# Queries and keys of the last nine blocks turned by DMA instead of by TensorE, in a fused attention and MLP kernel

## The chip, the cores and the metric

The kernel runs on one core of a Trainium2 chip. The metric is the time of one execution on the device, in microseconds (us). A kernel is timed in several runs; one execution is profiled as well. The engines' names are those of the profile: PE is TensorE's matmul side, PEld its weight loads, DVE is VectorE, ACT is ScalarE, POOL is GpSimd, SP is SyncE. In this kernel SP only issues DMAs, and POOL issues the loads and makes a few small vectors.

## The reference

Attention with a sliding window and a linear distance penalty, then a normalized MLP with a residual. There are 8 batches, 8 heads, 576 tokens and 64 dimensions a head.

```python
scores = scale * np.matmul(q, k.transpose(0, 1, 3, 2))
mask = (rel >= 0) & (rel < 128)                  # rel = query position - key position
scores = np.where(mask, scores + bias[None], -1000000000.0)   # bias = -slope_h * |rel|
...
attn = attn / (np.sum(attn, axis=-1, keepdims=True) + 1e-09)
out = np.matmul(attn, v)
...
xn = (x - mu) / np.sqrt(var + 1e-06) * g_ln      # x: heads joined, 512 wide
ch = np.maximum(xn @ w_ch1, 0.0) @ w_ch2         # 512 -> 2048 -> 512
return x + ch
```

## The kernel before

**Blocks.** The batches are taken in 4 pairs. The 576 tokens of a batch are four strips of 128 and a tail of 64. A pair has 9 blocks of 128 queries: two for each strip (one per batch) and one for both tails. `order` (L229) lists the 36 blocks, n = 9 * pair + block; "the last nine blocks" are n = 27 to 35, all of pair 3. The 36 blocks form groups for the MLP (`GROUPS`, L26): six groups of two blocks, then six of four.

**Turning.** A score matmul contracts over the 64 dimensions of a head, so q and k must lie with the dimensions on the partitions; two heads share the 128 partitions. `load_qk` (L207) has POOL issue the loads of a strip for both batches: the DMA converts to fp16 and puts pairs of neighbouring tokens side by side, so that one load has 512 pieces of 128 numbers. `turn` (L283) then has PE transpose 64x64 pieces against an identity (`transposed`, L267, the matmuls are on L277): 64 for a strip, 32 for a tail. They go to PSUM, from the ninth block on mostly to the two banks `ps_sc` that the scores use too, and DVE and ACT copy them to SBUF (L296, L297, for a tail L302), where keys come back to token order and queries keep all even tokens ahead of the odd ones. `turned_pool` has three buffers for q and three for k.

**Attention.** `scores` and `attend` (L367) compute a block's scores in 64x64 quadrants of PE (L393): j is the half of the array's rows (the head of a pair), c the half of its columns. Each of the 128 queries sees only the keys in its window, so `seen` (L353) leaves out halves of queries that no mask lets through; what stays in the bank from earlier is finite, and the mask makes it zero. Only for the first eight blocks is everything computed. ACT takes the exponential from PSUM (L401), DVE multiplies by the decayed mask (L412), PE multiplies by v with a column of ones (`values`, L431, matmuls on L445), and DVE divides by the sum (L454).

**Normalization.** From block 8 on, `stats` (L494) makes mean and variance on DVE (L542, L543) and the reciprocal deviation rstd on POOL (L497, L500); `normal` (L480), called centring here, subtracts the mean and multiplies by rstd on DVE (L484) and has SP issue a DMA transpose of the 128x512 block into the group's tile xT (L492).

**MLP.** `mlp1(g)` multiplies xT by the first weights (L677): 16 units of 128 hidden columns, 4 matmuls each; ACT (some on DVE) applies the maximum with zero (L693). `mlp2` (L701) is the second product for the small groups (L710). For groups 6 to 11 `fast_mlp2` (L747) does it with seven products of half size instead of eight (L776), with sums of hidden halves that DVE makes into the buffers `hsum` (L745); it has 14 units. DVE adds the residual, and SP stores the rows (`store`, L862).

**Order.** PE, DVE and ACT run in the order written by hand; the order of POOL is the scheduler's, and before the change SP's too. `steps` is a list of attention steps. For each block n from 8 on it holds four:

```python
steps.append(turn_step(n + 3, True) if ... order[n + 3][1] % 2 == 0 else [])
steps.append(step)        # loads ahead, values(n), scores(n + 2)
steps.append(masks + [(stats, n)])
steps.append([(normal, n)])
```

`weave_at` (L875) interleaves them with the units of the MLP: the numbers in its call say after which unit of that MLP the next step is issued. `mlp1(7)`, for instance, has steps after its units 0, 2, 5, 7, 8, 10, 13 and 15. While the MLP of a group runs, the attention is at the blocks of the next groups; the last steps end in group 10, and group 11 is MLP alone.

**Loads.** The raw q and k have four buffers each, and POOL runs ahead of the other engines: a strip's load is issued when the turn four strips earlier has read its buffer.

Of the kernel before, what the change touches and what calls it, by code (L numbers as in the profile page):

```python
# [10 lines left out]
FP16 = mybir.dt.float16  # L11
# [6 lines left out]
P = 128  # L18
# [9 lines left out]

NV = 10
AHEAD = 6  # L30

# [27 lines left out]
def kernel(  # L59
# [25 lines left out]
    raw_pool = pool("raw", 4)  # L85
    turned_pool = pool("turned", 3)
    probs_pool = pool("probs", 4)
# [41 lines left out]
    g_row = consts.tile([P, DM], FP32)  # L129
    one_line = consts.tile([1, P], FP32)  # L130
# [7 lines left out]
    w2 = consts.tile([P, NFB, DM], FP16)  # L138
    QF, QD = NFB // 2, DM // 2
    hsum = [consts.tile([P, QF, 2 * P], FP16, name=f"hs{i}", tag=f"hs{i}") for i in range(2)]  # L140
    spare = [w1[:, i, :].rearrange("p (f d) -> p f d", d=QD) for i in range(4)]
# [63 lines left out]
    raw = {}  # L205

    def load_qk(src, tag, p, i):  # L207

        n = min(P, S - i * P)
        t = raw_pool.tile([P, H, 2, D], FP16, tag=tag, name=tag)  # L210
        raw[tag, p, i] = t
        for b in range(2):
            nc.gpsimd.dma_start(  # L213
                out=t[b * n // 2 : (b + 1) * n // 2],
                in_=src[2 * p + b, :, i * P : i * P + n, :].rearrange(
                    "h (c r) d -> c h r d", r=2
                ),
            )
# [64 lines left out]
    def turn(p, i, in_sc=False, copies=(nc.vector.tensor_copy, nc.scalar.copy)):  # L283
# [3 lines left out]


        ps = [bank(b if in_sc else None) for b in range(2)]
        k = keys_tile("k", p, i)  # L290
        if i < 4:
            q = queries(p, i)
            transposed("q", p, i, [t[:, 0] for t in ps])
# [4 lines left out]
        else:  # L298
            q = keys_tile("q", p, i)
            for tag, t, dst, copy in zip("qk", ps, (q, k), copies):  # L300
# [10 lines left out]
    def queries(p, i):  # L311
        t = turned_pool.tile([P, 2, 2, HP, HALF], FP16, tag="q", name="q")
        turned["q", p, i] = t.rearrange("p b r h c -> p b h r c")
        return t
# [38 lines left out]
    def seen(p, blk, o, t):  # L353
# [13 lines left out]
    def attend(p, blk, keys, mask, tag, hps):  # L367
# [12 lines left out]
        else:  # L380
            pr = weights_of[p, blk][-1][0]
        banks = ps_sc[len(scored) % 2]
        scored.append((p, blk))
        ps = banks.rearrange("p j (n t q) -> p j n t q", n=len(hps), t=nk)
        qt, b = turned["q", p, blk // 2], blk % 2
        for n, hp in enumerate(hps):
            for t, o in enumerate(keys):
                kt = turned["k", p, o // 2][:, o % 2]
                for c, r, queries in seen(p, blk, o, t):
                    cols = slice(c * HALF, (c + 1) * HALF)  # L390
                    for j in range(2):
                        rows = slice(j * HALF, (j + 1) * HALF)
                        nc.tensor.matmul(  # L393
                            in_halves(ps[cols, j, n, t, :])[:, r, queries],
                            kt[rows, hp, cols],
                            in_halves(qt[rows, b, hp])[:, r, queries],
                            start=True,
                            stop=True,
                        )
        dst = pr[:, heads].rearrange("p h t q -> p h (t q)")  # L400
        nc.scalar.activation(  # L401
# [514 lines left out]
    assert done == len(steps)  # L916
# [30 lines left out]
```

## Time and profile before

| what | value |
| --- | --- |
| median of 3 runs | 323.09 us (323.06 to 325.91) |
| the profiled execution | 322.94 us |
| its span, first to last instruction | 321.1 us |
| granted TensorE clock, mean | 1.00 |
| busy: PE, DVE, ACT, POOL | 307.5, 233.4, 184.6, 114.9 us |
| transposes of q and k on PE (L277) | 528 + 512 to the score banks, 48 + 64 to others |
| transposes of xc by DMA (L492) | 28 |
| bytes by DMA | 32.34 MB in 102048 packets |

A row of the profile's groups gives line, engine, operation, the tiles written and read, and the count; then busy time and the mean of one in ns; then the engine's idle time just before, and what ended it. In a timeline a row is one or more instructions in a run: start and length in us, then what and how many. In a row of waits stand the total, the number of times and the longest. In a table of stages each engine's busy time is followed by its instruction count. "SPq" and "POOLq" are the queues of the two engines, with their DMA issues.

### The profile page before, as it was taken

To read this page: it belongs to the slowest core of one execution; us is meant where nothing else is said; L and a number is where in the kernel's file an instruction comes from. 1 tells how busy PE (TensorE), PEld (TensorE's weight loads), DVE (VectorE), ACT (ScalarE), POOL (GpSimd) and SP (SyncE) were. 2 spreads that over 40 slices of the span, in tenths; PEclk is the share of its full clock that TensorE was granted. 3 is DMA by queue.
4 is the path that set the end of the run, shared out by engine and by line. 5 is a ranking of instruction groups with operands and counts; after the bars stand their busy time and mean duration, and the time that the engine had idled before them with its cause. 6 is when DMAs were issued, how large, how long until landed. Compare 5 with 4: busy or idle time off the path is not lost.

```text
span 321.1 us, 10472 instructions
## 1 busy us (share of the span) xinstructions
PE 307.5 (96%) x4478; PEld 207.3 (65%) x4478; DVE 233.4 (73%) x556; ACT 184.6 (57%) x320; POOL 114.9 (36%) x188
## 2 busy tenths in 40 slices
PE   8889999999899999999999999999999999999993
PEld 2478655758558576545875587558755874685582
DVE  2788878786687788758994899579958984761462
ACT  6588756666558466478248824873488247405600
POOL 8833657769145264534252534220000001000000
PEclk9999999999999999999999999999999999999999
DMA  9999999999999899895389769660340134015005
GB/s 113 169 206 196 190 142 189 186 115 184 59 118 120 78 143 92 89 160 55 45 108 160 68 68 115 117 51 18 84 85 18 18 68 98 18 32 117 0 2 131
DMA packets 102048, 32.34 MB, mean 101 GB/s; under 512 B 92913, under 2 KB 97649, under 8 KB 102002
## 3 DMA queue, kind: packets, MB, share of 16 engines
q0 software_dynamic: 79872, 18.36, 66.7%
q1 hardware_dynamic: 21810, 13.05, 19.5%
q8 instruction: 35, 0.57, 0.8%
q10 hardware_dynamic: 320, 0.26, 0.4%
q14 instruction: 11, 0.09, 0.1%
HBM read 36.90 MB, written 9.44 MB: 144 GB/s over the span
## 4 chain that ended last, share of the span: by engine, by line
PE 76%; DVE 10%; ACT 5%; POOL 3%; DMA 2%; issue 2%; POOLq 0%; ACTq 0%
PE ps_r L677 24%; PE ps_r L776 21%; PE ps_m L710 10%; PE ps_m L677 9%; PE ps_sc L393 4%; ACT probs L401 3%; PE ps_sc L277 2%; PE ps_r L445 2%; DVE probs L412 2%; DMA k<-in_k_dram 2%; PE ps_pv L445 2%; DVE st L542 1%; POOL rstd L500 1%; POOL q L213 1%; DVE o L852 1%
## 5 line engine op out<-in xcount | busy, mean ns | idle before, releaser
L677 PEld LDWEIGHTS <-w1g 128*128 128x128 f16 x640 | 60.0, 98 | 48.9 <-issue 1.8
L677 PE MATMUL ps_r<-xT,w1g 128*128 128x512 f16 x384 | 85.5, 379 | 0.0
L401 ACT ACTIVATE probs<-ps_sc 128x1024 f16<-128x1024 f32 x56 | 54.3, 1027 | 35.5 <-PE ps_sc L393 35.5
L693 ACT ACTIVATE ht<-ps_r 128x512 f16<-128x512 f32 x96 | 56.2, 600 | 30.6 <-PE ps_r L677 30.4
L497 POOL TENSOR_TENSOR rstd<-moments,powers 128x1 f32<-128x1 f32 x28 | 5.4, 193 | 118.5 <-DVE moments L543 118.4
L710 PE MATMUL ps_m<-w,ht 128*128 128x512 f16 x192 | 46.0, 380 | 0.0
L776 PE MATMUL ps_r<-w,ht 128*128 128x256 f16 x384 | 44.1, 273 | 0.0
L223 POOL DMA_DIRECT2D vx<-in_v_dram x40 | 34.6, 879 | 22.4 <-PE ps_r L445 9.7
L412 DVE TENSOR_TENSOR probs<-probs,m 128x1024 f16<-128x1024 f16 x56 | 37.3, 688 | 6.5 <-ACT probs L401 6.3
L776 PEld LDWEIGHTS <-ht 128*128 128x128 f16 x384 | 37.1, 98 | 4.7
L693 ACT ACTIVATE ht<-ps_m 128x256 f16<-128x256 f32 x91 | 33.1, 388 | 8.6 <-PE ps_m L677 6.0
L213 POOL DMA_DIRECT2D q<-in_q_dram x40 | 27.4, 692 | 14.4 <-PE ps_sc L277 6.6
L677 PE MATMUL ps_m<-xT,w1g 128*128 128x256 f16 x256 | 31.4, 273 | 1.1 <-ACT ht L693 0.8
L213 POOL DMA_DIRECT2D k<-in_k_dram x40 | 26.8, 684 | 6.7 <-DMA w<-in_moe_w_ch_dram 3.1
L710 PEld LDWEIGHTS <-ht 128*128 128x128 f16 x192 | 17.1, 98 | 17.4
L484 DVE TENSOR_SCALAR xc<-x,moments,rstd 128x512 f16<-128x512 f16 x28 | 11.5, 412 | 20.0 <-POOL rstd L500 19.0
L542 DVE BATCH_NORM_STATS2 st<-x 128x6 f32<-128x512 f16 x36 | 24.6, 684 | 0.0
L393 PE MATMUL ps_sc<-q,k 64*64 64x128 f16 (+1 forms) x1088 | 20.2, 208 | 3.9 <-DVE k L297 1.3
L296 ACT COPY q<-ps_sc 128x512 f16<-128x512 f16 x15 | 8.8, 586 | 25.1 <-PE ps_sc L277 24.9
L776 PE MATMUL ps_r<-w,hs 128*128 128x256 f16 x192 | 22.5, 273 | 0.0
L445 PEld LDWEIGHTS <-probs 128*128 128x128 f16 x448 | 18.7, 97 | 4.7 <-DVE probs L412 0.3
L393 PEld LDWEIGHTS <-k 64*64 64x64 f16 x1088 | 15.2, 107 | 8.9 <-issue 6.5
(85 smaller groups left out, 390.7 us busy)
## 6 DMA issues: line engine op xcount, KB each, us to landing
out_dram<-o SPq DMA_DIRECT2D x68, 128.0 KB, 2.5
q<-in_q_dram POOLq DMA_DIRECT2D x32, 128.0 KB, 4.5
k<-in_k_dram POOLq DMA_DIRECT2D x32, 128.0 KB, 5.8
vx<-in_v_dram POOLq DMA_DIRECT2D x32, 128.0 KB, 7.6
w<-in_moe_w_ch_dram POOLq DMA_DIRECT2D x8, 512.0 KB, 12.2
q<-in_q_dram POOLq DMA_DIRECT2D x8, 64.0 KB, 4.8
k<-in_k_dram POOLq DMA_DIRECT2D x8, 64.0 KB, 4.3
vx<-in_v_dram POOLq DMA_DIRECT2D x8, 64.0 KB, 6.0
```

The costliest lines, as they stand in the source:

```text
L213: nc.gpsimd.dma_start(out=t[b * n // 2 : (b + 1) * n // 2], in_=src[2 * p + b, :, i * P : i * P + n, :].rearrange("h (c r) d -> c h r d", ...
L223: nc.gpsimd.dma_start(out=vx[p0 : p0 + n, :, 0:D], in_=v[b, :, t0 : t0 + n, :].rearrange("h p d -> p h d"),)
L393: nc.tensor.matmul(in_halves(ps[cols, j, n, t, :])[:, r, queries], kt[rows, hp, cols], in_halves(qt[rows, b, hp])[:, r, queries], start=Tr ...
L401: nc.scalar.activation(out=dst.rearrange("p (n j) q -> p j n q", j=2), in_=ps.rearrange("p j n t q -> p j n (t q)"), func=AF.Exp, scale=in ...
L412: nc.vector.tensor_tensor(out=dst, in0=dst, in1=mask, op=ALU.mult)
L445: nc.tensor.matmul(ps[:, i, :], pr[:, h, t, :], vext[(p * NSLOT + o) % NV][:, h, :], start=(n == 0), stop=(n == len(terms) - 1),)
L484: nc.vector.tensor_scalar(out=xc, in0=xs[order[n]], scalar1=moments[:, n, 0:1], scalar2=rstd[:, n : n + 1], op0=ALU.subtract, op1=ALU.mult,)
L542: nc.vector.bn_stats(out=st, in_=xs[order[n]])
L677: nc.tensor.matmul(ps[:, 0:cols], w[:, kb, fb * P : (fb + 1) * P], xT[:, kb, 0:cols], start=(kb == 0), stop=(kb == NKB - 1),)
L693: nc.scalar.activation(out=ht[:, fb, 0:cols], in_=ps[:, 0:cols], func=AF.Relu)
L710: nc.tensor.matmul(sums[at], ht[:, fb, at * P : (at + 1) * P], w2[:, fb, :], start=(fb == 0), stop=(fb == NFB - 1),)
L776: nc.tensor.matmul(banks[name][pair][:, pair, :], lhs[:, fb, pair * P : (pair + 1) * P], rhs[:, fb, :], start=(first and fb == 0 and (pair ...
```

## The change

For pair 3 (`by_dma(p)`, p >= 3) the loads lay q and k out with tokens on partitions and the heads of a batch side by side, and `turn` has SP issue DMA transposes straight into the turned tiles: two for q and two for k of a strip, one each for the tails, 18 in all. No transposes on PE, no PSUM and no copies are used for them. A strip's q is loaded by four DMAs (even tokens to partitions 0 to 63, odd ones to 64 to 127), so that the queries come in the same order as before, its k by two; pieces are now 64 numbers long.

The turn's place in the steps changes for all pairs: it was the first step of block n + 1, behind the centring of block n; now it stands between `stats(n)` and `normal(n)`. A turn by DMA is issued one block earlier still (n + 5 beside n). SP is under the written order too. A few places of the weave are shifted by one to four units.

`junk` notes for each score bank that transposes were put there; the next scores in that bank compute everything for row half j = 0, which is the half that shares its bank with them. For this the loop over j now stands outside the loop over the columns' halves, in all blocks. `turned_pool` has four buffers instead of three, and the two tiles with g's values are put into the memory of `hsum`.

```diff
@@
+BY_DMA_TURN = 3
...
-    turned_pool = pool("turned", 3)
+    turned_pool = pool("turned", 4)
...
-    g_line = consts.tile([1, DM], FP32)
...
+    g_line, g_row = (
+        t.rearrange("p f d -> p (f d)")[:, 0 : 2 * DM].bitcast(FP32) for t in hsum
+    )
+    g_line = g_line[0:1]
...
+    def by_dma(p):
+        return p >= BY_DMA_TURN
+
     def load_qk(src, tag, p, i):
...
+        if by_dma(p):
+            t = raw[tag, p, i] = t.rearrange("p h r d -> p (h r d)").rearrange(
+                "p (b h d) -> p b h d", b=2, h=H
+            )
+            for b in range(2):
+                rows = src[2 * p + b, :, i * P : i * P + n, :]
+                if i == 4:
+                    parts = [(t[b * n : (b + 1) * n, 0], rows)]
+                elif tag == "k":
+                    parts = [(t[:, b], rows)]
+                else:
+                    rows = rows.rearrange("h (c r) d -> h r c d", r=2)
+                    parts = [
+                        (t[r * HALF : (r + 1) * HALF, b], rows[:, r]) for r in range(2)
+                    ]
+                for dst, part in parts:
+                    nc.gpsimd.dma_start(out=dst, in_=part.rearrange("h p d -> p h d"))
+            return
...
+        k = keys_tile("k", p, i)
+        q = queries(p, i) if i < 4 else keys_tile("q", p, i)
+        if by_dma(p):
+            for tag, dst in (("q", q), ("k", k)):
+                src = raw.pop((tag, p, i))
+                for b in range(2 if i < 4 else 1):
+                    t = dst[:, b]
+                    if tag == "q" and i < 4:
+                        t = turned["q", p, i][:, b].rearrange("p h r c -> p h (r c)")
+                    nc.sync.dma_start_transpose(
+                        out=t, in_=src[:, b].rearrange("p h d -> p (h d)")
+                    )
+            return
...
+        junk[sc] = True
...
+    junk = [False, False]
...
-        if p == 0 and blk < SEEN:
+        if whole or p == 0 and blk < SEEN:
             return [(0, both, every), (1, both, every)]
...
-                for c, r, queries in seen(p, blk, o, t):
-                    cols = slice(c * HALF, (c + 1) * HALF)
-                    for j in range(2):
-                        rows = slice(j * HALF, (j + 1) * HALF)
+                for j in range(2):
+                    rows = slice(j * HALF, (j + 1) * HALF)
+                    for c, r, queries in seen(p, blk, o, t, junk[at] and j == 0):
+                        cols = slice(c * HALF, (c + 1) * HALF)
...
+        junk[at] = False
...
+    def turn_at(n):
+        ahead = [m for m in (n + 3, n + 4) if m < count and order[m][1] % 2 == 0]
+        return [
+            f
+            for m in ahead
+            if by_dma(order[m][0]) == (m == n + 4)
+            for f in turn_step(m, True)
+        ]
+
+    steps.append(turn_at(8))
     for n in range(8, count):
         first_half, second_half = values_steps(n)
-        steps.append(
-            turn_step(n + 3, True) if n + 3 < count and order[n + 3][1] % 2 == 0 else []
-        )
...
+        if n + 1 < count:
+            steps.append(turn_at(n + 1))
         steps.append([(normal, n)])
...
-    with tc.manual_schedule(engines={engine.PE}):
+    with tc.manual_schedule(engines={engine.PE, engine.SP}):
...
-            weave_at(mlp2(3), 0, 1, 1, 2, 4, 4, 5, 6)
+            weave_at(mlp2(3), 0, 1, 1, 3, 4, 4, 5, 6)
...
-            weave_at(mlp2(4), 0, 2, 2, 3, 5, 7, also=(1, 4, 6))
-            weave_at(mlp1(5), 0, 1, 4, 8, 10, 12, also=(3, 6, 9))
+            weave_at(mlp2(4), 0, 2, 2, 5, 5, 7, also=(1, 4, 6))
+            weave_at(mlp1(5), 0, 5, 5, 8, 10, 12, also=(3, 6, 9))
...
-                weave_at(fast_mlp2(g), 1, 3, 6, 7, 7, 9, 12, 13)
+                weave_at(fast_mlp2(g), 1, 3, 6, 7, 7, 10, 12, 13)
```

More of the change, by code (lines that the diff above doesn't have):

```diff
@@ L126 @@
     nc.sync.dma_start(out=g_sb, in_=moe_g_ln.rearrange("(kb p) -> p kb", p=P))
-    g_line = consts.tile([1, DM], FP32)
+    QF, QD = NFB // 2, DM // 2
+    hsum = [consts.tile([P, QF, 2 * P], FP16, name=f"hs{i}", tag=f"hs{i}") for i in range(2)]
+    g_line, g_row = (
+        t.rearrange("p f d -> p (f d)")[:, 0 : 2 * DM].bitcast(FP32) for t in hsum
+    )
+    g_line = g_line[0:1]
     nc.sync.dma_start(out=g_line, in_=moe_g_ln.rearrange("(o d) -> o d", o=1))
-    g_row = consts.tile([P, DM], FP32)
     one_line = consts.tile([1, P], FP32)
@@ L138 @@
     w2 = consts.tile([P, NFB, DM], FP16)
-    QF, QD = NFB // 2, DM // 2
-    hsum = [consts.tile([P, QF, 2 * P], FP16, name=f"hs{i}", tag=f"hs{i}") for i in range(2)]
     spare = [w1[:, i, :].rearrange("p (f d) -> p f d", d=QD) for i in range(4)]
@@ L283, in turn @@
     def turn(p, i, in_sc=False, copies=(nc.vector.tensor_copy, nc.scalar.copy)):
+        k = keys_tile("k", p, i)
[11 more added lines that the diff above has]
+            return
         ps = [bank(b if in_sc else None) for b in range(2)]
-        k = keys_tile("k", p, i)
         if i < 4:
-            q = queries(p, i)
             transposed("q", p, i, [t[:, 0] for t in ps])
@@ L298, in turn @@
         else:
-            q = keys_tile("q", p, i)
             for tag, t, dst, copy in zip("qk", ps, (q, k), copies):
@@ L311, in queries @@
     def queries(p, i):
+        if by_dma(p):
+            t = turned_pool.tile([P, 2, HP, 2, HALF], FP16, tag="q", name="q")
+            turned["q", p, i] = t
+            return t
         t = turned_pool.tile([P, 2, 2, HP, HALF], FP16, tag="q", name="q")
@@ L348, with seen @@
     weights_of, unmasked, scored = {}, {}, []
+    junk = [False, False]
     def in_halves(t):
         return t if len(t.shape) == 3 else t.rearrange("p (r c) -> p r c", r=2)
-    def seen(p, blk, o, t):
+    def seen(p, blk, o, t, whole):
         both, every = slice(0, 2), slice(0, HALF)
         first, second = slice(0, HALF // 2), slice(HALF // 2, HALF)
-        if p == 0 and blk < SEEN:
+        if whole or p == 0 and blk < SEEN:
             return [(0, both, every), (1, both, every)]
@@ L381, in attend @@
             pr = weights_of[p, blk][-1][0]
-        banks = ps_sc[len(scored) % 2]
+        at = len(scored) % 2
+        banks = ps_sc[at]
         scored.append((p, blk))
```

## The prediction

> **What bounds the kernel now.** I read the profile page first, then busy time by stage, then the chain of waits.
>
> ```profile
> span 321.1 us, 10472 instructions
> ...
> PE 307.5 (96%) x4478; PEld 207.3 (65%) x4478; DVE 233.4 (73%) x556; ACT 184.6 (57%) x320; POOL 114.9 (36%) x188
> ```
> ```profile
> 75.00:135.00 60.00, 56.84 (x1002) 38.89 (x1002) 45.39 (x108) 36.79 (x71) 29.17 (x49) 1.00 1.02 106
> 135.00:190.00 55.00, 54.24 (x730) 35.70 (x729) 43.26 (x93) 33.83 (x50) 21.15 (x36) 1.00 1.02 97
> 190.00:256.00 66.00, 65.86 (x1057) 46.15 (x1056) 53.72 (x117) 38.13 (x56) 12.46 (x25) 1.00 0.42 64
> ```
>
> The stage rows give the window, then busy time of PE, PEld, DVE, ACT and POOL, the granted clock, and the DMA share. PE is the bound, and most strictly so where the change works: from 190 to 256 us it idles 0.14 us of 66, at a granted clock of 1.00. From 135 to 190 it idles 0.76 us, from 75 to 135 it idles 3.16 us. So in the last pair a microsecond taken off PE is a microsecond off the end, and elsewhere at most those idle times can be won. "x32" of a PE row is a count of matmuls.
>
> **The turns that leave PE.** The chain of waits runs through all five turns of pair 3; busy time by stage, cut at their starts and ends and for the transposes' line alone (window, PE busy, PEld busy, clock, DMA):
>
> ```profile
> 190.06:190.71 0.65, 0.65 (x64) 0.53 (x64) 1.00 0.00 0
> ...
> 253.55:254.17 0.62, 0.62 (x32) 0.51 (x32) 1.00 0.00 0
> sum 3.33, PE 3.25 PEld 2.70; mean PE 0.65 PEld 0.54
> ```
>
> Four turns of 64 transposes and the tail's 32 (288 in all) take 3.3 us, other matmuls standing right before and behind. All of it goes: **-3.3 us**. With them go nine copies each from DVE and ACT; I give these nothing, because neither engine is the bound after 190 us (DVE is busy 53.72 of 66 us there, ACT 38.13) and PE covers them.
>
> **Waits behind the copies.** After a turn the next scores need its PSUM banks back. These are PE's longest waits from 75 to 135 us, then those from 135 to the end (total, times, longest), and the chain into one of them (start, duration).
>
> ```profile
> PE ps_m L677 <- ACT ht L693: 0.8, 2, 0.5
> PE ps_sc L393 <- DVE k L297: 0.7, 1, 0.7
> PE ps_sc L393 <- DVE rec L453: 0.6, 1, 0.6
> ```
> ```profile
> PE ps_sc L393 <- DVE rec L453: 0.4, 1, 0.4
> PE ps_sc L393 <- DVE k L297: 0.4, 1, 0.4
> ```
> ```profile
> 163.40 0.57 POOL rstd L500
> ...
> 164.00 0.41 DVE xc L484
> ...
> 165.53 0.42 DVE q L296
> 165.94 0.65 DVE k L297
> ```
>
> The chain shows the cause: on DVE the centring (xc) stands ahead of the turn's copies and itself waits for POOL's rstd. The change swaps the two: the copies fill the time in which rstd is made, and turns that stay on PE in pair 2 come two or three units of MLP earlier (a unit is one 128-column slice of hidden, or a quarter of an output block, some 0.9 us) while the scores stay where they were. So both late waits should go: **-0.8 us**. Of the early 0.7 + 0.6 = 1.3 us I take nine tenths, **-1.2 us**, and not more, because PE's other wait there, 0.8 us for ACT's ht, has nothing to do with the copies and is late next. Bounds: none of it, or all 3.16 us idle.
>
> **More scores on PE.** After a turn through the score banks the first scores in each bank now compute all columns in row half 0 (j = 0). Nine such turns remain on PE behind block 8. Pair 0 already computes all columns in both halves; a block of it beside one of pair 2, each with the row that follows it:
>
> ```profile
> 41.46 0.64 PE L393 MATMUL ps_sc<-q,k 64*64 64x128 f16 x32
> 42.04 1.04 PE L710 MATMUL ps_m<-w,ht 128*128 128x512 f16 x4
> ```
> ```profile
> 198.39 0.54 PE L393 MATMUL ps_sc<-q,k 64*64 64x64 f16 x32
> 198.86 0.60 PE L677 MATMUL ps_r<-xT,w1g 128*128 128x512 f16 x2
> ```
>
> Start to next start: 0.58 against 0.47 us, so 0.11 more for both halves. For one half it lies between 0.05 and 0.11; the halves run side by side, so I take 0.09: 9 x 0.09 = **+0.8 us**.
>
> The loops are also turned round, for every block: the four 64x64 quadrants were visited column by column, alternating row halves; now row half 0 twice, then row half 1 twice. Nothing in before runs scores so. But the transposes of a full turn are written in exactly the new order, and 64 of them take 0.65 us, 10 ns each, so the order does not keep quadrants from running together. A tail turn stays in one row half, and there 32 take 0.62 us, 19 ns each. The bounds for the order are thus nothing and, where short matmuls wait for long ones as if all were long, 28 blocks (n from 8) x 0.11 = 3.1 us. I take **+0.5 us**, near the row of the full turn. Sharing g's rows with the hidden sums' buffer, and one turned buffer more, add no instruction, and g's last reader is block 3's centring, long before the first hidden sum: 0. SP's other DMAs keep their order: 0. Of the weave's other places only block 9's values and block 11's scores come later, by one unit, with other matmuls to fill it: 0.
>
> [...]
>
> **What the new path costs: POOL, SP, DMA.** These queues are hidden behind PE unless they come too late. The rows (the landing row is that of xT's 28 transposes, the last two are two of them being issued on SP):
>
> ```profile
> L223 POOL DMA_DIRECT2D vx<-in_v_dram x40 | 34.6, 879 | 22.4 <-PE ps_r L445 9.7
> ...
> L213 POOL DMA_DIRECT2D q<-in_q_dram x40 | 27.4, 692 | 14.4 <-PE ps_sc L277 6.6
> ...
> q<-in_q_dram POOLq DMA_DIRECT2D x32, 128.0 KB, 4.5
> ...
> vx<-in_v_dram POOLq DMA_DIRECT2D x32, 128.0 KB, 7.6
> ```
> ```profile
> 132.97 1.42 POOL L213 DMA_DIRECT2D q<-in_q_dram  x2 [0.89 <-PE ps_sc L277]
> ...
> 138.85 0.25 POOL L497 TENSOR_TENSOR rstd<-moments,powers 128x1 f32<-128x1 f32 x1
> ```
> ```profile
> DMA to landing us min/median/max: 2.4/3.6/7.5
> ```
> ```profile
> 88.31 1.20 SPq L492 DMA_TRANSPOSE xT<-xc  x1
> ```
> ```profile
> 158.36 1.19 SPq L492 DMA_TRANSPOSE xT<-xc  x1
> ```
>
> POOL: a full turn's loads are now four of q with 512 pieces each (priced as the old q load, 0.69 us) and two of k in the shape of v's (0.88): 4.5 us instead of 4 x 0.69 = 2.8, so +1.7 us four times, about 7 us with the tail. Queued behind them is rstd: the one at 138.85 stands behind the loads that begin at 132.97 and would come up to 1.7 us later, still for a block of the group whose MLP starts at 167. Cost 0; if DVE, which waits in order for rstd, has nothing else to do, up to 1.7 us per turn.
>
> Loads lead by far: those from 132.97 are of block 27, which is turned at 190 now and near 176 after; even 7.6 us to land, v's median, leaves over 25 us.
>
> [...]
>
> SP: 18 transposes more at 1.2 us are 21.6 us of queue, in bursts of 4.8 us, put ahead of the transposes of xc for blocks 22, 24, 26, 28 and 30 and of the stores behind them. None of these is the last of its group of four, so each has several units left. A turn's own readers, scores of block 27 say, stand 19 units (some 17 us) behind its issue; 4.8 + 7.5 = 12.3 us at the slowest landing. Cost 0.
>
> **Centring comes one place later.** The MLP of a group needs its last block's xT. The transposes quoted above from 88.31 and 158.36 are the last ones of the groups of blocks 8-9 and 16-19; the matmuls that read them begin here:
>
> ```profile
> 94.99 1.26 PE L677 MATMUL ps_m<-xT,w1g 128*128 128x256 f16 x9
> ```
> ```profile
> 167.11 1.25 PE L677 MATMUL ps_r<-xT,w1g 128*128 128x512 f16 x5
> ```
>
> There are 6.7 and 8.7 us from issue to need, less 3.6 us median landing: 3 and 5 us to spare. Moved behind a turn's two DVE copies (1.07 us) or three units (2.6 us, of which DVE lags some already), they still fit. Cost 0; if not, the difference, in each of six groups.
>
> **Sum.** -3.3 - 0.8 - 1.2 + 0.8 + 0.5 = -4.0 us. The profiled execution took 322.94 us (span 321.1 and 1.8 around it), 0.15 under the median 323.09, so it stands for it: **318.9 us**.
>
> **Rivals.**
> *A, the gain is given back in PE itself:* order and extra columns at their upper bounds, 3.1 + 1.0, and no early wait won: 322.94 - 3.3 - 0.8 + 4.1 = 322.9. Against it, the full turn's 10 ns. A half of this, about 321, is more probable than all.
> *B, slower:* the new order makes scores run as the tail turn does, one row half at a time. If a block's 0.47 us doubles, 28 blocks add 13 us: 318.4 + 13 = 331. It makes the kernel slower than before from 0.16 us a block (4.5 / 28). For it: 19 ns in the tail's turn; against it: the full turn, in the same order. [...]
> *C, a new wait for xT or rstd:* a burst on SP together with a landing of 7.5 us makes the last xT of a group late, 3.9 us past the median and 1.5 of place, so about 0.5 us past the 5 to spare, and more as PE gets ahead by 4; three groups of the last pair at 1 us: about 322. For it: DVE is 53.72 busy of 66 us. Against: after 190 us the DMA share is 0.42, less than half of that before it.
> *D, the transposes were covered anyway:* excluded by 0.14 us idle.
>
> **Numbers.** Forecast 0.60; A 0.18; B 0.08; C 0.14. One per cent, 3.2 us, is about what a measurement tells from no change: faster means under 319.9. The forecast's case spreads from 316.0 (order free, columns at 0.05, all 3.16 idle won: 322.94 - 3.3 - 0.8 - 3.2 + 0.5 = 316.1) to 319.9; A and C lie in 320 to 323, half of B is over 326. So faster 0.59, same 0.31, slower 0.10, range 316.0 to 322.6.
>
> **What would show it.** In the profile after: no transposes of q and k on PE for the last nine blocks and PE time from 190 us to the end shorter by 3.3; 18 more transposes on SP of about 1.2 us; no wait of scores for k's copy; scores of pairs 1 to 3 start to start at 0.47 to 0.50, and 0.56 right after a turn. Scores of 0.6 us or more in all blocks would make B true; PE waiting for the xT DMA, or PE idle behind a centring that waits for rstd, would make C true. The forecast is wrong at its first term if PE idles over 1 us in the last pair.

## The result and the profile after

| what | before | after |
| --- | --- | --- |
| median, first comparison (6 runs each) | 323.41 us | 319.86 us (318.48 to 320.81) |
| ratio | | 0.9878, interval 0.9837 to 0.9919 |
| median, repeated with the experiments | 324.11 us (11 runs) | 319.42 us (6 runs, 318.27 to 320.43) |
| ratio | | 0.9849, interval 0.9819 to 0.9880 |
| profiled execution, span | 322.94, 321.1 us | 320.09, 318.3 us |

The forecast was 318.9 us, in a range of 316.0 to 322.6. The profiled execution after is 2.85 us shorter than the one before, where the sum said 4.0. Ratios leave out a run that is over 1.5% above the fastest of its kernel; of all runs told of here this is one, of two_pairs_pool. In the new kernel the scores are on L434, the transposes of q and k on L301 (PE) and L322 (DMA), the centring on L526 with its DMA transpose on L534, rstd on L539 and L542, the first MLP product on L728, the second on L761 and L827. ACT's maximum is on L744, the copies of the turns on L331 and L332, the moments on L585, the division on L495 and L496, DVE's sums of the second product on L845 and L903, the loads that POOL issues on L234, L237 and L247. The page and the table of stages (window, then PE, PEld, DVE, ACT and POOL, then clock, DMA share and GB/s):

```profile
span 318.3 us, 9920 instructions
...
PE 304.7 (96%) x4190; PEld 205.4 (65%) x4190; DVE 228.9 (72%) x547; ACT 179.4 (56%) x311; POOL 124.7 (39%) x196
```
```profile
0.00:20.00 20.00, 15.73 (x262) 7.52 (x263) 9.27 (x39) 12.78 (x27) 15.88 (x25) 0.91 1.43 153
...
75.00:135.00 60.00, 56.65 (x985) 38.77 (x984) 46.13 (x107) 37.65 (x73) 29.97 (x50) 1.00 1.00 102
135.00:190.00 55.00, 55.00 (x761) 36.15 (x760) 43.06 (x92) 33.89 (x50) 31.03 (x47) 1.00 1.39 114
190.00:256.00 66.00, 66.00 (x807) 46.73 (x805) 52.67 (x117) 34.75 (x49) 12.48 (x23) 1.00 0.59 89
```

PE has 288 matmuls fewer, as it should, and from 135 to 256 us it never idles: the late waits are gone. From 75 to 135 us it still idles 3.35 us, before it was 3.16. And the clock in the first 20 us reads 0.91, where it was 1.00. These are PE's longest waits from 75 to 135 us in the kernel after:

```profile
PE ps_m L761 <- ACT ht L744: 1.2, 1, 1.2
PE ps_m L728 <- DVE x L496: 0.9, 1, 0.9
PE ps_m L728 <- ACT ht L744: 0.6, 2, 0.3
PE ps_m L728 <- DMA xT<-xc: 0.4, 1, 0.4
```

No score waits there for k's copy any more, which was the purpose of the swap, but other waits of the same size have come, among them one for xT. Where the time went is seen best from landmarks. The table gives the time from the first MLP matmul of one group to that of the next, read from the timeline of PE in each trace ("again" is a second profile of the unchanged new kernel; the kernels to the right are those of the experiments below):

| groups | before | after | again | swap_only | dma_only | dma_only_pool | pool_written | before_pool |
| --- | --- | --- | --- | --- | --- | --- | --- | --- |
| 3 to 4 | 19.72 | 19.39 | 19.35 | 19.55 | 19.79 | 18.56 | 17.52 | 18.47 |
| 4 to 5 | 19.66 | 20.50 | 20.58 | 20.32 | 19.74 | 19.74 | 19.89 | 19.67 |
| 5 to 6 | 20.23 | 20.14 | 20.13 | 20.13 | 20.18 | 20.18 | 20.11 | 20.22 |
| 6 to 7 | 32.23 | 31.55 | 31.56 | 31.56 | 32.46 | 32.45 | 31.56 | 32.24 |
| 7 to 8 | 31.75 | 31.02 | 31.01 | 31.95 | 39.60 | 31.02 | 31.01 | 32.12 |
| 8 to 9 | 31.72 | 29.96 | 29.96 | 31.58 | 29.96 | 29.97 | 29.96 | 32.00 |
| 9 to 10 | 31.67 | 30.20 | 30.20 | 31.85 | 30.19 | 30.19 | 30.20 | 31.70 |
| start of group 0 | 19.50 | 20.81 | 19.18 | 19.12 | 21.12 | 21.27 | 19.34 | 19.80 |

The reader is to see three things. The last pair (7 to 10) gives 3.96 us, the same to 0.02 us in every kernel of the table that turns it by DMA, with the one exception of 39.60. The groups 3 to 6 give nothing: 59.61 us before, 60.03 after. And the start varies by some 2 us (19.12 to 21.27) between kernels that run the same matmuls there.

### The profile page after: what moved, and what is told of

The parts are those of the page before. It is cut to its first block, busy times and chain, and to the rows that moved or that the text cites. A ratio compares the mean times of both kernels' runs of the same rounds, so it can differ in the third digit from the quotient of the medians.

```text
span 318.3 us, 9920 instructions
## 1 busy us (share of the span) xinstructions
PE 304.7 (96%) x4190; PEld 205.4 (65%) x4190; DVE 228.9 (72%) x547; ACT 179.4 (56%) x311; POOL 124.7 (39%) x196
## 4 chain that ended last, share of the span: by engine, by line
PE 84%; DVE 5%; POOL 3%; ACT 2%; DMA 2%; issue 2%; POOLq 0%; ACTq 0%
PE ps_r L728 26%; PE ps_r L827 23%; PE ps_m L761 11%; PE ps_m L728 10%; PE ps_sc L434 5%; PE ps_r L487 3%; PE ps_sc L301 2%; PE ps_pv L487 2%; ACT probs L443 2%; DMA k<-in_k_dram 2%; POOL q L237 1%; DVE o L903 1%; DVE x L496 1%; PE ps_warm L283 1%; DVE probs L454 1%
## 5 line engine op out<-in xcount | busy, mean ns | idle before, releaser
L728 PEld LDWEIGHTS <-w1g 128*128 128x128 f16 x640 | 60.4, 98 | 50.5 <-DVE x L496 1.8
L728 PE MATMUL ps_r<-xT,w1g 128*128 128x512 f16 x384 | 85.1, 379 | 0.0
L744 ACT ACTIVATE ht<-ps_r 128x512 f16<-128x512 f32 x96 | 56.2, 600 | 31.6 <-PE ps_r L728 31.5
L761 PE MATMUL ps_m<-w,ht 128*128 128x512 f16 x192 | 46.0, 380 | 1.2 <-ACT ht L744 1.2
L539 POOL TENSOR_TENSOR rstd<-moments,powers 128x1 f32<-128x1 f32 x28 | 6.8, 243 | 102.4 <-DVE moments L585 102.4
L827 PE MATMUL ps_r<-w,ht 128*128 128x256 f16 x384 | 44.1, 273 | 0.0
L247 POOL DMA_DIRECT2D vx<-in_v_dram x40 | 34.7, 884 | 22.3 <-PE ps_r L487 9.0
L827 PEld LDWEIGHTS <-ht 128*128 128x128 f16 x384 | 37.1, 98 | 4.8
L744 ACT ACTIVATE ht<-ps_m 128x256 f16<-128x256 f32 x91 | 32.9, 391 | 8.6 <-PE ps_m L728 6.2
L728 PE MATMUL ps_m<-xT,w1g 128*128 128x256 f16 x256 | 31.5, 273 | 2.2 <-DVE x L496 0.9
L761 PEld LDWEIGHTS <-ht 128*128 128x128 f16 x192 | 17.1, 98 | 18.7 <-issue 1.3
L237 POOL DMA_DIRECT2D q<-in_q_dram x30 | 20.5, 692 | 19.3 <-PE ps_sc L301 10.6
L237 POOL DMA_DIRECT2D k<-in_k_dram x30 | 20.2, 686 | 4.8 <-DMA w<-in_moe_w_ch_dram 3.5
L434 PE MATMUL ps_sc<-q,k 64*64 64x128 f16 (+1 forms) x1088 | 20.5, 210 | 1.5 <-ACT probs L443 1.1
L827 PE MATMUL ps_r<-w,hs 128*128 128x256 f16 x192 | 21.9, 273 | 0.0
L827 PEld LDWEIGHTS <-hs 128*128 128x128 f16 x192 | 18.8, 98 | 2.2
L845 DVE TENSOR_TENSOR o<-ps_r,x 128x512 f32<-128x512 f32 x24 | 16.5, 686 | 4.3 <-PE ps_r L827 4.3
L434 PEld LDWEIGHTS <-k 64*64 64x64 f16 x1088 | 15.2, 108 | 6.8 <-issue 4.6
```

The source lines that it names most:

```text
L237: nc.gpsimd.dma_start(out=t[b * n // 2 : (b + 1) * n // 2], in_=src[2 * p + b, :, i * P : i * P + n, :].rearrange("h (c r) d -> c h r d", ...
L247: nc.gpsimd.dma_start(out=vx[p0 : p0 + n, :, 0:D], in_=v[b, :, t0 : t0 + n, :].rearrange("h p d -> p h d"),)
L434: nc.tensor.matmul(in_halves(ps[cols, j, n, t, :])[:, r, queries], kt[rows, hp, cols], in_halves(qt[rows, b, hp])[:, r, queries], start=Tr ...
L728: nc.tensor.matmul(ps[:, 0:cols], w[:, kb, fb * P : (fb + 1) * P], xT[:, kb, 0:cols], start=(kb == 0), stop=(kb == NKB - 1),)
L744: nc.scalar.activation(out=ht[:, fb, 0:cols], in_=ps[:, 0:cols], func=AF.Relu)
L761: nc.tensor.matmul(sums[at], ht[:, fb, at * P : (at + 1) * P], w2[:, fb, :], start=(fb == 0), stop=(fb == NFB - 1),)
```

## The experiments

My theory after the result was: the five turns give what they were priced at, the swap of turn and centring gives the late waits, and the early waits are kept by POOL, because the scheduler put loads of q and k between a centring's moments and its rstd. The rivals: that the price lies in the new loop order or the extra columns, and that the place of the turn is itself what makes the new waits.

**The DMA turns alone (dma_only).** The turns stand again behind the preceding centring, and the weave has its old places.

```diff
-        if n + 1 < count:
-            steps.append(turn_at(n + 1))
         steps.append([(normal, n)])
+        if n + 1 < count:
+            steps.append(turn_at(n + 1))
```

> Pair 3 is turned by DMA as in the changed kernel, but every turn stands behind the preceding block's centring again, with the old places of the weave. Theory (PE is full from 135 us on, so what leaves PE leaves the end): the five turns give 3.3 us, the drain of the matmuls ahead of each some 0.1 us more, and the scores that compute all columns cost 0.7 us; the waits for k's copies in pair 2 (0.8 us) come back. About 1.0 us slower than the changed kernel, near 320.8 us, and 2.6 us faster than before. Rival (the swapped order earned the gain, the transposes were mostly covered): over 322 us.

Measured: 327.14 us (326.08 to 329.9), ratio 1.0104 (1.0072 to 1.0136). This theory fell: with the turns by DMA but in the old place the kernel is slower than before. The whole loss stands in one interval, 7 to 8. The rival's number came true, but not its reason: 8 to 10 is as short as in the new kernel, so the transposes were not covered. PE's only wait in 190 to 256 us, then the timeline of POOL and of SP, two links of the chain of waits, and the timeline of DVE in the stretch ahead of it (start, length):

```profile
PE ps_r L827 <- DVE o L845: 5.9, 1, 5.9
```
```profile
187.07 1.80 POOL L234 DMA_DIRECT2D k<-in_k_dram  x2
191.23 1.38 POOL L234 DMA_DIRECT2D q<-in_q_dram  x2 [2.36 <-DMA q<-q]
196.81 1.36 POOL L234 DMA_DIRECT2D k<-in_k_dram  x2 [4.20 <-DMA k<-k]
198.17 0.22 POOL L539 TENSOR_TENSOR rstd<-moments,powers 128x1 f32<-128x1 f32 x1
```
```profile
187.07 2.61 SPq L322 DMA_TRANSPOSE k<-k  x2
```
```profile
188.35 7.89 DMA k<-k
196.25 0.02 issue
```
```profile
191.30 0.18 DVE L585 BATCH_NORM_AGGREGATE moments<-st 128x2 f32<-128x6 f32 x1
191.40 0.66 DVE L845 TENSOR_TENSOR o<-ps_r,o 128x512 f32<-128x512 f32 x1
191.97 0.68 DVE L796 TENSOR_TENSOR ht<-ht 128x1024 f16<-128x1024 f16 x1
199.06 0.41 DVE L526 TENSOR_SCALAR xc<-x,moments,rstd 128x512 f16<-128x512 f16 x1 [6.41 <-POOL rstd L542]
199.39 1.28 DVE L845 TENSOR_TENSOR o<-ps_r,x 128x512 f32<-128x512 f32 x2
```

Read from the bottom: the sum o waits behind a centring on DVE, the centring waits for rstd, and rstd stands on POOL behind a k load. The moments it needs were there at 191.5. The k load waits because its raw buffer is still being read by the DMA turn that SP issued at 187.07 to 189.7 and whose last transpose landed at 196.2, 7.9 us after its issue. A load waits for a landing now, not for PE, and everything behind it on POOL waits too. The chain costs 8.6 us against the other kernels (39.60 - 31.02), of which 5.9 are the wait. The rest is the clock, which fell while PE was idle (0.84 over the window from 196 to 200 us, PE busy 0.00 there); windows of the same trace, from the end of the wait on (window, PE busy, clock, DMA share, GB/s):

```profile
200.00:202.00 2.00, 1.87 (x9) 0.50 0.85 91
202.00:204.00 2.00, 2.00 (x11) 0.50 0.67 42
204.00:206.00 2.00, 2.00 (x13) 0.61 0.21 45
206.00:208.00 2.00, 2.00 (x21) 1.00 0.97 207
```

Half of 4 us and 0.39 of 2 us make 2.8 us; with 5.9 that is 8.7.

**The swap alone (swap_only).** All turns stay on PE; order, columns, place and weave are those of the new kernel.

```diff
-BY_DMA_TURN = 3
+BY_DMA_TURN = 4
```

> No pair is turned by DMA; order, places, extra columns and buffers are those of the changed kernel. Theory: the waits of pairs 2 and 3 behind the copies go (about 1.2 us), the extra columns cost 0.7 us, and the stretch from 75 to 135 us is 0.2 to 0.6 us longer: within 0.5 us of before, 322.9 to 323.6 us, and the scores in the trace start to start at 0.477 us as before. Rival (the swapped order earned the gain): under 321.5 us.

Measured: 323.52 us (322.99 to 324.92), ratio 1.0002 (0.9982 to 1.0023). As the theory has it: without the DMA the change gives nothing. From 6 to 7 it gains 0.67 us, the two late waits less the columns; from 7 to 10 it loses 0.24, columns less a few small waits; and from 3 to 6 it loses 0.39, where PE's waits are the new ones:

```profile
PE ps_m L761 <- ACT ht L744: 1.2, 1, 1.2
PE ps_m L728 <- DVE x L496: 0.7, 1, 0.7
PE ps_m L728 <- ACT ht L744: 0.6, 2, 0.3
PE ps_m L728 <- DMA xT<-xc: 0.5, 1, 0.5
```

So they come with the swap and not with the DMA turns. Ahead of these intervals 2 to 3 is 0.63 us longer than before (21.01 against 20.38), and the start 0.38 us earlier.

**Without the extra columns (no_whole).** The scores after a turn leave out what they left out before; the new loop order stays.

```diff
-                    for c, r, queries in seen(p, blk, o, t, junk[at] and j == 0):
+                    for c, r, queries in seen(p, blk, o, t, False):
```

> The changed kernel, but the first scores after a turn leave out the columns that no mask lets through, as the kernel before did; the loops keep their new order. Theory: eight blocks go from 0.566 to 0.477 us (0.516 to 0.477 where half of a block is meant), 0.6 us less in all, of which the 0.3 us after 135 us reach the end: 0.3 to 0.7 us faster than the changed kernel. Rival (PE has room there): no difference, under 0.1 us.

Measured: 318.32 us (317.56 to 318.77), ratio 0.9834 (0.9798 to 0.9871), 1.5 us under the new kernel and more than expected. Its profile has no low clock at the start and begins group 0 at 19.25 us instead of 20.81, which is as much as the whole difference. From there to group 10 it needs 0.25 us more, not less (238.99 against 238.74): from 6 to 8, where the theory had the gain, it wins 0.30 us; ahead of that it loses 1.06 us between groups 0 and 4 and wins 0.50 from 4 to 6, and no run here shows why. So the median's 1.5 us are not the columns' price. The scores themselves, after a turn, in the new kernel and in this one:

```profile
184.57 0.63 PE L434 MATMUL ps_sc<-q,k 64*64 64x128 f16 x32
185.13 1.05 PE L827 MATMUL ps_r<-w,ht 128*128 128x256 f16 x8
```
```profile
183.35 0.54 PE L434 MATMUL ps_sc<-q,k 64*64 64x128 f16 x32
183.83 1.37 PE L827 MATMUL ps_r<-w,ht 128*128 128x256 f16 x11
```

Start to next start it is 0.56 and 0.48 us, so this block's columns cost 0.08 to 0.09. Over the nine blocks that have them it is 0.04 to 0.19, mostly 0.09, and 0.80 us in all. And the 0.48 with the new order is what blocks in before had with the old one (0.47 in the prediction's row): the loop order costs nothing.

**POOL in written order (pool_written).**

```diff
-    with tc.manual_schedule(engines={engine.PE, engine.SP}):
+    with tc.manual_schedule(engines={engine.PE, engine.SP, engine.Pool}):
```

> The changed kernel with POOL in written order too, so that the loads of a block come in their step and rstd never stands behind loads that the scheduler put ahead of it. Theory (between 75 and 135 us the gain was given back because rstd of blocks 9 and 10 stands behind loads of q and k on POOL, and with it DVE's centring, the adds behind it and xT): the stretch from the first matmul of group 4's MLP to that of group 5 falls from 20.5 to under 19.8 us, PE no longer waits for the xT DMA, and the time falls by 0.8 to 1.5 us. Rival (ACT's ht is what PE waits for there, and would be with any order on POOL): the stretch stays at 20.3 us or more and the time within 0.3 us.

Measured: 316.34 us (315.97 to 316.69), ratio 0.9775 (0.9741 to 0.981). The theory holds, and the gain is larger than expected. The timeline of POOL in the new kernel shows what the scheduler's order did:

```profile
88.59 1.43 POOL L237 DMA_DIRECT2D q<-in_q_dram  x2 [6.93 <-PE ps_sc L301]
90.02 0.22 POOL L539 TENSOR_TENSOR rstd<-moments,powers 128x1 f32<-128x1 f32 x1
90.15 0.70 POOL L237 DMA_DIRECT2D k<-in_k_dram  x1
90.86 0.58 POOL L542 TENSOR_TENSOR rstd<-rstd,powers 128x1 f32<-128x1 f32 x1
```

The centring that follows, on DVE:

```profile
87.03 0.18 DVE L585 BATCH_NORM_AGGREGATE moments<-st 128x2 f32<-128x6 f32 x1
88.60 0.42 DVE L331 COPY q<-ps_sc 128x512 f16<-128x512 f16 x1 [1.39 <-PE ps_sc L301]
88.94 0.72 DVE L332 COPY k<-ps_sc 128x512 f16<-128x512 f16 x1
91.48 0.41 DVE L526 TENSOR_SCALAR xc<-x,moments,rstd 128x512 f16<-128x512 f16 x1 [1.82 <-POOL rstd L542]
```

The moments are ready at 87.2, but the first half of rstd stands behind two q loads that wait 6.93 us for PE's turn, and its second half behind a k load as well: rstd is ready at 91.44. DVE stands still for 1.82 us at the centring, and the divisions x, the masks and the next sums behind it come late. With POOL in written order rstd stands ahead of the loads:

```profile
85.69 0.18 POOL L539 TENSOR_TENSOR rstd<-moments,powers 128x1 f32<-128x1 f32 x1 [3.04 <-DVE moments L585]
85.95 0.57 POOL L542 TENSOR_TENSOR rstd<-rstd,powers 128x1 f32<-128x1 f32 x1
```

It waits for nothing but its moments. The interval 3 to 4 falls from 19.39 to 17.52 us, 4 to 5 from 20.50 to 19.89, the table's others stay to 0.03: 2.5 us, all of it where the new waits were; the medians' difference of 3.5 holds the start as well. PE's wait for xT and the one of 1.2 us are gone.

**The DMA turns alone, POOL in written order (dma_only_pool).** Both edits, that of dma_only and that of pool_written.

> The turns of the last pair by DMA in the place of before (behind the preceding strip's centring), and POOL's queue in the order in which the kernel is written. Theory Q: the kernel with the DMA turns alone lost its time in POOL's queue. There the raw k load of a strip stood ahead of an rstd and waited 4.2 us for the DMA turn of the strip before (7.9 us from issue to landing), the centring waited 6.4 us for that rstd, the last sum of the MLP waited for the centring and PE 5.9 us for that sum. With rstd ahead of the load in the written order that wait is gone: 317 to 319.5 us, no wait of PE over 1 us behind 190 us. Rival T: the later place of the turn itself is at fault (k lands too late for its scores, or xT stands behind the turn on SP): still 322 us or more, and PE waits in the last pair for a DMA or for xT.

Measured: 319.24 us (317.86 to 320.12), ratio 0.987 (0.9844 to 0.9895). Theory Q holds: the interval 7 to 8 is 31.02 instead of 39.60, and PE waits for nothing from 190 to 256 us. The 7.9 us that dma_only lost were thus POOL's queue. What is left of the old place against pool_written is 2.9 us in the medians, in part the start (21.27 against 19.34 us in the profiles). In the table the old place costs 1.04 us in 3 to 4, and 0.89 in 6 to 7, where the old late waits are back:

```profile
PE ps_sc L434 <- DVE rec L495: 0.4, 1, 0.4
PE ps_sc L434 <- DVE k L332: 0.4, 1, 0.4
```

Four of the kernels that turn the last pair by DMA also price the swap, with its places in the weave, from 3 to 6: with POOL in written order it wins 0.96 us (58.48 in dma_only_pool, 57.52 in pool_written), with the scheduler's order it costs 0.32 (59.71 in dma_only, 60.03 in the new kernel).

**POOL in written order in the old kernel (before_pool).**

```diff
-    with tc.manual_schedule(engines={engine.PE}):
+    with tc.manual_schedule(engines={engine.PE, engine.Pool}):
```

> The kernel before with nothing changed but POOL's queue in the order in which the kernel is written. Theory N: POOL's order was spoiled by the change alone, since only the kernel after shows the rstd of the sixth and seventh centring between q and k loads. Then nothing is gained: 322.8 to 324. Rival O: the old kernel's own waits of PE between 75 and 135 us (3.16 us of idle) are to a good part of the same origin, and go as they went in the changed kernel with POOL in written order (1.17 us of idle): 321 to 322.

Measured: 323.12 us (322.4 to 324.48), ratio 0.999 (0.9969 to 1.001). By the number, theory N. By the trace, part of O: 3 to 4 is 1.25 us shorter here too, but 7 to 9 is 0.65 longer and groups 2 to 3 lose 0.56. So not only the change spoiled POOL's order: in before the rstd of block 8 stands behind two v loads (moments ready at 78.18, rstd begun at 79.25), and in written order it starts at once. What gives the gain back is for the most part scores that wait for k's copy: 0.9 us in three waits from 135 to 290 us, where before has 0.4 in one. The swap takes such waits away (swap_only has none there), and in pair 3 the DMA turns do too: dma_only_pool, without the swap, loses nothing in 7 to 9.

**Both gains (pool_no_whole).** pool_written and no_whole together.

> The changed kernel with POOL in written order and with the masked columns left out after a turn as in the kernel before. Theory: the two gains are of different engines and places and add: 316.34 less 0.7 (nine strips' worth of the columns' 0.07 us each, as the scores' start-to-start shows) to 1.5 (the difference of the two runs' medians): 314.8 to 315.6. Rival: the extra columns cover work of another engine, then 316 or more.

Measured: 316.04 us (315.65 to 317.52), ratio 0.9779 (0.9755 to 0.9804). The medians of this and of pool_written differ by 0.3 us, which the intervals cannot tell from nothing or from 0.7. By the number the rival came true (316 or more). The traces tell more: from the first MLP matmul of group 0 to that of group 10 this kernel needs 0.64 us less (235.45 against 236.09), near the theory's lower value.

**Two pairs by DMA (two_pairs_pool).** pool_no_whole with BY_DMA_TURN = 2.

> As the kernel with POOL in written order and without the extra columns, and with the q and k of the last two pairs of heads turned by DMA instead of one. Theory: the price of a turn on PE holds for the second pair as well: five strips of two times 0.65 / 2 us and 0.1 us for the change of tile size, 0.74 us each, so 3.7 us less: 311.3 to 312.5. Rival L: in the pair before the last PE waits for other engines part of the time, and so only part of it is seen: 312.5 to 314.5. Rival W: the DMA turns meet the q, k and v loads of the queue and POOL's order once more: slower than 315.5.

Measured: 320.04 us (317.11 to 321.91), ratio 0.9873 (0.9837 to 0.9909): rival W. Its profiled execution is the slowest of the six and shows one wait of 5.6 us of the first MLP product, which the profile puts down to a store. It may as well be the xT transpose just ahead of that store on SP: it was issued at 130.77, landed 7.6 us later, and the wait ends at 138.51. The rows are that wait, the time from issue to landing of this kernel's DMA turns (least, median, most), and the same of the new kernel's:

```profile
PE ps_r L728 <- DMA out_dram<-o: 5.6, 1, 5.6
```
```profile
DMA to landing us min/median/max: 2.4/6.2/8.3
```
```profile
DMA to landing us min/median/max: 2.4/2.4/5.2
```

Even its fastest run is slower than pool_no_whole's median, so the turns of pair 2 do not pay in this place. Of the 6.07 us between the two profiles 1.80 are the start, and 5.00 the intervals 5 to 7, with that wait and a clock of 0.50 behind it, from 138 to 144 us; 7 to 8 is 0.73 shorter, one turn's price. No other execution of this kernel was profiled, so it is not shown that the others have the wait, nor how much of it is the landing and how much the order on SP and POOL.

**The start (after_again, after_fill, pool_no_whole_fill).** after_again is the new kernel unchanged. The others put four warming matmuls, whose result nobody reads, between the q and the k transposes of the second strip.

```diff
             transposed("q", p, i, [t[:, 0] for t in ps])
+            if in_sc:
+                warm(fill.pop())          # fill: 4 for the first strip that comes here, then 0
             transposed("k", p, i, [t[:, 1] for t in ps])
```

> The changed kernel once more, nothing altered, to see whether its slow start belongs to it. In its first profile PE waited 0.42, 0.23 and 0.79 us for the q and k loads of the second strip, the granted clock read 0.62 and 0.53 in the slices from 14 to 18 us, and the first MLP began at 20.81 us; the kernel with POOL in written order has the same PE, SP and POOL instructions up to there, waited 0.29 and 0.77 us, kept a clock of 1.00 and began at 19.34 us. Theory S (the start varies by execution, with the landing of the loads): the profile may show either start; the runs spread over 2 us or so, 318.3 to 321, median 319 to 320.2. Rival (the change itself delays the start): always 0.91 in the first 20 us, and the runs lie together.

> The changed kernel with four more of its warming matmuls (0.245 us each at full clock) between the q and the k transposes of the second strip, where PE waits for the k load. They compute nothing that is used. Theory S: the idle before k that brings the lower clock is filled, the clock stays at 1.00, the first MLP begins at 19.3 to 19.8 us, and the median falls to 318.2 to 319.2 with a narrower spread. Rival: the clock drops all the same, or the four matmuls (1.0 us) come on top, 319.9 to 321.

> The same four warming matmuls in the fastest kernel so far (POOL in written order, no extra columns), whose profile had a clock of 1.00 at the start already. Theory S: the lowest time stays at 315.6 and the highest (317.52) comes down, median 315.6 to 316.0. Rival: the four matmuls are on the path, 316.5 to 317.

Measured: after_again 319.42 us (318.27 to 320.43), and its profile, at 318.27, has a clock of 1.00 in the first 20 us; after_fill 318.70 (318.51 to 319.64), ratio 0.9838 (0.9811 to 0.9864); pool_no_whole_fill 315.50 (315.36 to 316.83), ratio 0.9731 (0.9705 to 0.9758). PE's timeline of the first profile, then its windows, then the windows of the second:

```profile
12.21 0.44 PE L301 MATMUL ps_sc<-iden,q 64*64 64x64 f16 x30 [0.42 <-DMA q<-in_q_dram]
12.88 0.22 PE L301 MATMUL ps_sc<-iden,k 64*64 64x64 f16 x2 [0.23 <-DMA k<-in_k_dram]
13.88 0.44 PE L301 MATMUL ps_sc<-iden,k 64*64 64x64 f16 x30 [0.79 <-DMA k<-in_k_dram]
```
```profile
12.00:14.00 2.00, 0.78 (x46) 1.00 2.22 153
14.00:16.00 2.00, 2.00 (x42) 0.62 1.23 186
16.00:18.00 2.00, 2.00 (x28) 0.53 1.23 204
```
```profile
12.00:14.00 2.00, 1.21 (x73) 1.00 2.08 170
14.00:16.00 2.00, 2.00 (x34) 1.00 1.36 203
```

In the traces theory S holds. The same program lands its second strip's loads 0.4 us sooner or later (PE goes on with k at 13.45 or 13.88 us); PE waits 0.8 or 1.4 us; in the later case the clock reads 0.62 and 0.53 in the two windows from 14 to 18 us (1.7 us are lost in them) and group 0 starts 1.6 us later (20.81 against 19.18). The fill takes this away in after_fill: its profile begins group 0 at 19.13 us, four of its six runs lie within 0.2 us of the lowest, and the spread falls from 2.2 to 1.1 us. The intervals of the two ratios overlap, so the runs' times alone do not show the gain of 0.7 us. The fill does not cover the first strip: the slowest run of pool_no_whole_fill, which is its profiled one, has 0.91 again, after a wait of 0.5 us for the first strip's k. By its median that last kernel is the fastest of all that ran.

## Why the prediction was right, and where it was wrong

**The turns, forecast -3.3 us.** Right, and a little small. From 7 to 10 the new kernel needs 3.96 us less than before and 4.20 less than swap_only, which has the same order, place and columns but turns on PE. Some 0.5 of the 4.20 are the extra columns that follow turns on PE (five blocks, 0.04 to 0.19 each), so the turns' leaving gives 3.7 us, 0.74 each where I had 0.65. The 0.65 was the transposes' own busy time. The rest stands ahead of the turn, in the timeline of before:

```profile
187.28 2.78 PE L776 MATMUL ps_r<-w,hs 128*128 128x256 f16 x24
189.99 0.45 PE L277 MATMUL ps_sc<-iden,q 64*64 64x64 f16 x32
...
194.32 3.66 PE L776 MATMUL ps_r<-w,ht 128*128 128x256 f16 x32
197.81 0.65 PE L445 MATMUL ps_r<-vx,probs 128*128 128x65 f16 x16
```

Start to next start, 24 matmuls of the second product take 2.71 us ahead of 64x64 transposes; 32 take 3.49 us ahead of 128x128 matmuls, which is 2.62 for 24. So the turn costs 0.09 us there; ahead of a turn in the first product it is 0.09 as well (5.28 us for 24 from 198.86, against 6.92 for 32 from 207.76, which is 5.19 for 24). My expectation of dma_only calls this a drain; the traces show the time, not what makes it. The forecast would have been wrong here if PE idled in the last pair: it idles 0.00 of 66 us. The copies that left DVE and ACT gave nothing seen, as said.

**The late waits, forecast -0.8.** Right: the interval 6 to 7, which holds both, is 0.89 us shorter without the columns (31.34 in no_whole) and 0.67 with them; dma_only, which has the old place, has neither gain.

**The early waits, forecast -1.2.** Wrong, and this is the step that failed. The named waits went, but groups 3 to 6 need 0.42 us more than before. The extra columns are not all of that: leaving them out wins 0.20 us there (60.03 to 59.83 in no_whole, 57.52 to 57.33 with POOL in written order). So of the waits nothing was won, and some 0.2 us lost. I had written of the queue that is to blame, "if DVE, which waits in order for rstd, has nothing else to do, up to 1.7 us per turn", and then priced POOL at 0, because I looked at how long the new loads are and not at where the scheduler would put them. The order of POOL is not written by hand; with the turn a place earlier the scheduler put q and k loads between the moments and rstd, as the new kernel, swap_only and no_whole have it there and dma_only, with the old place, has not. It is rival C, a new wait for rstd and xT, but in the old loads of the early groups and not in the last pair, where I had looked for it. pool_written wins 2.5 us from 3 to 6, but 1.25 of that come in the old kernel too (before_pool). The rest, some 1.3 us, is what the change lost through POOL: the swap is worth 0.96 us with POOL in written order, not far from the 1.2 forecast, and costs 0.32 with the scheduler's. So the reading of the copies was right, and the step that failed is the price of nothing for POOL.

**Extra columns, forecast +0.8.** Right: 0.04 to 0.19 a block and 0.80 us of PE's work over nine blocks; 0.64 us of it shows between groups 0 and 10 in the two kernels that differ by them alone (pool_written and pool_no_whole).

**Loop order, forecast +0.5.** Too high: 0.0, the scores take 0.48 us in both orders. The 318.4 from which rival B is counted is the forecast without this 0.5. Rival B, which needed a dearer order, falls with it; so does A, which needed both upper bounds.

**Centring later, SP, 0 each.** For the last pair right: no wait of PE there, and the DMA turns land within 5.2 us. dma_only shows how near the edge this was: the same DMA turns one place later cost 8.6 us through POOL, and the place that the change chose keeps rstd clear of them.

**The sum.** The profile of after_again, with an undisturbed start, took 318.27 us, 4.67 less than before's 322.94, against a forecast of 4.0. Of this 3.96 are the last pair, 0.67 the interval 6 to 7 and 0.32 the start; the groups 3 to 6 take 0.45 back, and the remainder is under 0.2. The first profile, 320.09, lost 1.3 us against before by a start with a lower clock, which no term of the sum had. So the forecast lies right in part by luck, because sizes were off that nearly cancel: the early waits came to +0.2 instead of -1.2, while the turns gave 0.4 more, the loop order cost 0.5 less, and late waits and columns were together 0.2 to 0.3 better; of the rest 0.32 us are the start and 0.16 stand behind group 11's first matmul, which no term had.

## What to carry to other kernels

In dma_only a load that waited 4.20 us for its buffer held up all that stood behind it on POOL: the rstd next in the queue began 6.7 us after its moments were ready. So when a step is moved, read the new order of every engine that a scheduler orders, and look for small operations on the critical chain behind such a load. That load waited for the landing of a DMA turn that read the buffer, 7.9 us after its issue (in the new kernel the DMA turns land after 2.4 to 5.2 us): where a transposition goes from PE to a DMA, put the loads into its buffer behind what is urgent. Edits that meet in one queue are to be tried together too: here each alone gave nothing or a loss (swap_only 1.0002, before_pool 0.999, dma_only 1.0104), and all three together 0.9775.

## What the runs showed of the hardware

In the new kernel's first profile, waits of PE of 1.44 us within 2.1 us, with short matmuls between them, came ahead of a granted clock of 0.62 and 0.53 in the next two windows of 2 us, while 0.8 us of waits in after_again and 1.06 in pool_written did not. The length of the waits alone does not decide it: in pool_no_whole_fill one of 0.5 us came ahead of three warming matmuls of 1.46 us together (from 9.12; three take 0.82 us in the new kernel, from 8.04), with 0.91 in the first 20 us, and in before_pool 1.2 us did not (1.00). What does decide it no run here shows. During dma_only's wait of 5.9 us the clock fell (0.84 from 196 to 200 us), and it stayed low until near 206 us (0.50, 0.50 and 0.61 from 200 to 206, then 1.00). The waits of the new kernel's two profiles differ by 0.65 us, the starts of their first MLP matmul by 1.6 us (20.81 against 19.18).
